# Another order for the chunk loop of a state-space and SwiGLU kernel, with a second adding transfer and phases read in order

## The chip, the cores and the metric

The kernel runs on one core of a Trainium2 chip. Time is device time in microseconds (us) for one launch; the median of several runs is compared, and a lower one is better. One further execution of each kernel was profiled, and all rows of traces come from it.

The engines work at their own pace and meet through semaphores: PE (TensorE, matrix products; PEld is its weight load), DVE (VectorE, elementwise), ACT (ScalarE, functions such as exp and sin), POOL (GpSimd; here mostly the issuer of DMA transfers) and SP (SyncE, the issuer of most transfers). Each executes its own instructions strictly in the order in which the program gives them.

## The reference

Two layers, each a diagonal state-space convolution and a SwiGLU block, with residuals:

```python
def _A_ref(u, A_re, A_im, B_re, B_im, C_re, C_im, log_dt, Dskip):
    dt = jnp.exp(log_dt)[:, None]
    A, Bc, Cc = A_re + 1j * A_im, B_re + 1j * B_im, C_re + 1j * C_im
    logdA, dB = dt * A, dt * Bc
    P = jnp.exp(logdA[:, :, None] * l[None, None, :])       # l = 0 .. L-1
    K = jnp.einsum("dn,dnl,dn->dl", Cc, P, dB).real
    ...                                                     # y = causal convolution of u with K
    return y + u * Dskip
for _ in range(2):
    x = x + _A_ref(_layernorm(x), ...)
    n = _layernorm(x)
    x = x + (silu(n @ w_gate) * (n @ w_up)) @ w_down
```

L = 2048 positions, D = 512 channels, N = 128 states, F = 1376. The kernel K (2048 lags for 512 channels) is the same in both layers.

## The kernel before

**Stages.** The head (0 to about 76 us) loads the inputs, makes the turns (phases as integers, a full turn being 2^32), normalizes the first block and transforms it, and prepares chunks 0 and 1. A loop over eight chunks of 64 channels (to about 300 us) makes K. What follows, some 900 us, splits the weights into halves of 16 bits, convolves in the frequency domain and runs the SwiGLU blocks; the change does not touch it.

**A chunk.** The powers for a lag are written as a product of a *large factor* (`re`, `im`: 65 columns for each channel, made by `gen_exp`, `gen_turns`, `gen_trig`, `gen_e`) and a *factor* `g` with 32 rows for each channel (`gen_g`). `lags` multiplies them on PE into `pk`; ACT copies `pk` out (`spread_in`, L499), transfers spread it over the partitions (`spread`), and `spectra` transforms it on PE, with copies on ACT (L550, L551), a sum on DVE (L553) and stores.

- `gen_turns` (DVE, L380 to L386): `xz` by a shift, then `tu`, 16 x 64 integers, by shifts and doubling sums. `gen_upper` (L407) adds the sixteenth row to all of `tu` in place, for the upper half.
- `gen_trig` (ACT): `xz` first, then the lower half (columns 33 to 48 of `re` and `im`: L399 the absolute value, L400 the sine, L401 the cosine), then, behind L407, the upper half (49 to 64) with the same three lines. L407 overwrites what the lower L399 and L400 read.
- `gen_exp` (ACT, L415 to L431): the moduli `mz` and the first 33 columns of `re`. `upper` (ACT, L425) squares them into `mu`.
- `gen_e` (DVE), seven steps: L440 twice, L443 twice, L445, L448 twice. The lags wait for the last.
- `gen_g` (DVE): L455 scales `xz`; L459 to L463 make row 0; then five doublings, each a product into the new rows (L469), a product into `tmp` (L480), and a sum (L483). The last doubling, 16 to 32, leaves its sum to a transfer in chunks 1 to 6: a product into `acc` (L472), then `G.dma_start(..., accum_op=OP.add)` (L473), issued by POOL, adds 1 MB to `g`. `acc` lies in the buffer of the other `g` (tags `ga` and `gb`), which the next chunk's `g` takes.

`take(it, n)` runs n steps of such a generator. In the head the order is written out. In the loop, each chunk c has a start on a list of moments (`starts`), and `prepare(c + 2)`, `factors(c + 1)`, `use(c)`, `second_block` (the first layer's second block, L289 on PE, L292 on ACT) and `weights` (sizes of the weights: loads by POOL at L317, squares on ACT at L323, column sums on PE, maxima on DVE at L329) put their steps on it with `at`. The list is sorted by moment and the instructions are given in that order; the moments only order them. PE, DVE, ACT and, in the loop, SP take this order as it is.

In the old order of one repetition, with `t` the chunk's start, DVE has: L455 to L460 (t + 0.2), L440 (0.3), L553 of the last chunk (2.1), the doublings with the second L440 in between (2.2 to 11.2, ending with L472), L380 to L386 for chunk c + 2 (14.4), L553 (17.3), L407 (21.5), then both L443, L445 and both L448 (22.0). ACT has: L425 (0.2), L499 (7.1), squares (8.0), `gen_exp` (12.6), L550 and L551 (14.0), squares (14.5), `xz` (17.4), L292 (17.6), the lower half (19.6), the upper (21.8), L593 (25.0), L550 and L551 (25.2).

Of the kernel before, what the change touches and what calls it, by code (L numbers as in the profile page):

```python
# [14 lines left out]
I32 = mybir.dt.int32  # L15
AF = mybir.ActivationFunctionType
OP = mybir.AluOpType
# [4 lines left out]
L, D, F = 2048, 512, 1376  # L22
P = 128
# [11 lines left out]
DC = 64  # L35
NCH = D // DC
# [37 lines left out]
def kernel(ctx, tc, x, a_re, a_im, b_re, b_im, c_re, c_im, log_dt, d_skip,  # L74
                           w_gate, w_up, w_down, c_ef, c_ei, c_ek, c_am, c_eh, c_eih, out):
    nc = tc.nc
    V, A, G, PE = nc.vector, nc.scalar, nc.gpsimd, nc.tensor
# [9 lines left out]
    def tl(shape, name, tag, dt=F32):  # L87
        return sb.tile(shape, dt, name=name, tag=tag, bufs=BUFS[tag])
# [106 lines left out]
    def stats(src, rows, scale, tag="stats", between=None, then=None):  # L195

        st = tl([P, 4, 6], "st", tag)
        mv = tl([P, 4, 2], "mv", tag)
        rs = tl([P, 8], "rs", tag)
        nb = rs[:, 4:]  # L200
        for r in range(rows):
            if between and r == 2:
                between()
            V.bn_stats(st[:, r], src[:, r])
            V.bn_aggr(mv[:, r], st[:, r])
        V.tensor_scalar(rs[:, :rows], mv[:, :rows, 1], EPS, 1.0 / scale ** 2, OP.add, OP.mult)
        G.tensor_tensor(rs[:, :rows], rs[:, :rows], mhalf[:, :rows], OP.pow)
        if then:
            then()
        V.scalar_tensor_tensor(nb[:, :rows], mv[:, :rows, 0], -1.0, rs[:, :rows], OP.mult, OP.mult)  # L210
        return rs, nb
# [147 lines left out]
        return re, im, mu, xz, mz, tu  # L359


    def turn_units(c0, c1):


        n = c1 - c0
        cs = slice(c0, c1)
        ft = tl([P, 2, 2, n], "ft", "sg")
        fr, fk = ft[:, 0], ft[:, 1].bitcast(I32)
        for i, scale in enumerate((1.0, 32.0)):
            V.scalar_tensor_tensor(fr[:, i], th[:, cs], scale / (2.0 * math.pi), dt[:, cs], OP.mult, OP.mult)  # L370
        A.activation(fk, fr, AF.Copy)
        V.tensor_tensor(fr, fr, fk, OP.subtract)
        for i, o in enumerate((th, th32)):
            V.tensor_scalar(o[:, cs].bitcast(I32), fr[:, i], TURN, TURN / 2 - 128.0, OP.mult, OP.min)

    def gen_turns(ch, ts):

        re, im, mu, xz, mz, tu = ts
        cs = slice(ch * DC, (ch + 1) * DC)
        V.tensor_tensor(xz[:, 1].bitcast(I32), th[:, cs].bitcast(I32).unsqueeze(1).to_broadcast([P, 5, DC]),  # L380
                        am.unsqueeze(2).to_broadcast([P, 5, DC]), OP.logical_shift_left)
        V.tensor_tensor(tu[:, 0:2], th32[:, cs].bitcast(I32).unsqueeze(1).to_broadcast([P, 2, DC]),
                        am[:, 0:2].unsqueeze(2).to_broadcast([P, 2, DC]), OP.logical_shift_left)
        yield
        for n in (2, 4, 8):
            V.tensor_tensor(tu[:, n:2 * n], tu[:, 0:n], tu[:, n - 1:n].to_broadcast([P, n, DC]), OP.add)  # L386
            yield
        G.memset(im[:, :, 32], 0.0)
        yield

    def gen_trig(ts):


        re, im, mu, xz, mz, tu = ts
        A.activation(xz[:, 2], xz[:, 1].bitcast(I32), AF.Sin, scale=-TWO_PI / TURN)
        tv = tu.rearrange("p m d -> p d m")
        for c, s, turns in ((xz[:, 0], xz[:, 1], xz[:, 1].bitcast(I32)), (re[:, :, 33:49], im[:, :, 33:49], tv),
                            (re[:, :, 49:65], im[:, :, 49:65], tv)):
            A.activation(c, turns, AF.Abs)  # L399
            A.activation(s, turns, AF.Sin, scale=TWO_PI / TURN)  # L400
            A.activation(c, c, AF.Sin, scale=-TWO_PI / TURN, bias=hpi)  # L401
            yield

    def gen_upper(ts):

        tu = ts[5]
        V.tensor_tensor(tu, tu, tu[:, 15:16].to_broadcast([P, 16, DC]), OP.add)  # L407
# [43 lines left out]
    def gen_g(ch, ts, g):  # L451

        re, im, mu, xz, mz, tu = ts
        w_ = w0[:, :, ch * DC:(ch + 1) * DC]
        V.tensor_tensor(xz, xz, mz.unsqueeze(1).to_broadcast([P, 3, 5, DC]), OP.mult)  # L455
        yield
        tmp8 = spare[0][:, :16 * DC].rearrange("p (i b d) -> p i b d", i=2, d=DC)
        tmp = tmp8
        V.tensor_tensor(g[:, :, 0], w_, re[:, :, 64].unsqueeze(1).to_broadcast([P, 2, DC]), OP.mult)  # L459
        V.tensor_tensor(tmp[:, :, 0], w_[:, ::-1], im[:, :, 64].unsqueeze(1).to_broadcast([P, 2, DC]), OP.mult)  # L460
        yield
        V.tensor_tensor(g[:, 0, 0], g[:, 0, 0], tmp[:, 0, 0], OP.subtract)
        V.tensor_tensor(g[:, 1, 0], g[:, 1, 0], tmp[:, 1, 0], OP.add)  # L463
        for n in (1, 2, 4, 8, 16):
            yield
            lv = n.bit_length() - 1
            zr = xz[:, 0:1, lv:lv + 1]
            zi = xz[:, 1:3, lv:lv + 1]
            V.tensor_tensor(g[:, :, n:2 * n], g[:, :, 0:n], zr.to_broadcast([P, 2, n, DC]), OP.mult)  # L469
            if n == 16 and 0 < ch < NCH - 1:  # L470
                tmp = tl([P, 2, 16, DC], "acc", ("gb", "ga")[ch % 2])
                V.tensor_tensor(tmp, g[:, ::-1, 0:16], xz[:, 2:0:-1, lv:lv + 1].to_broadcast([P, 2, 16, DC]), OP.mult)  # L472
                G.dma_start(g[:, :, 16:32].rearrange("p i b d -> p i (b d)"), tmp.rearrange("p i b d -> p i (b d)"),  # L473
                            accum_op=OP.add)
                continue
            step = min(n, 8)
            for b0 in range(0, n, step):
                tmp = tmp8[:, :, :step]
                o = slice(n + b0, n + b0 + step)
                V.tensor_tensor(tmp, g[:, :, b0:b0 + step], zi.to_broadcast([P, 2, step, DC]), OP.mult)  # L480
                if b0 + step == n:
                    yield
                V.tensor_tensor(g[:, :, o], g[:, :, o], tmp[:, ::-1], OP.add)  # L483
        yield
# [130 lines left out]
    def take(it, n):  # L615
        for _ in range(n):
            next(it, None)
# [302 lines left out]
    ts = [None] * (NCH + 2)  # L920
# [15 lines left out]
    with tc.manual_schedule(engines={mybir.EngineType.Activation, mybir.EngineType.DVE, mybir.EngineType.PE}):  # L936
# [2 lines left out]

        def turns():  # L940
            V.tensor_tensor(rho, rho, dt, OP.mult)
            turn_units(0, P)
            take(ex, 14)
            take(gen_turns(0, ts[0]), 5)
        stats_x = stats(xe, 4, 1.0, between=turns)
        tr = gen_trig(ts[0])
        take(tr, 2)
        gen_upper(ts[0])
        take(tr, 1)
        take(ex, 11)  # L950
        turn_units(P, D // 2)
        turn_units(D // 2, D)
        gen_w()
        norm_early(xe, ne, stats_x)
        fw = [direct(0, h, q, [ne[:, c, h * HD:(h + 1) * HD] for c in range(4)]) for h in range(2) for q in QORD]
        for f in fw:
# [7 lines left out]
        upper(ts[0])  # L964
        take(fw[0], 1)
        take(fw[1], 1)
        stats_x = stats(x1, 4, 1.0)
        take(fw[2], 1)
        for g in (gg, ge, gg, ge, gg, ge, gg, ge, gg, tn, gg, tn, gg, tn, gg, tn, gg, tn):
            take(g, 1)  # L970
        tr = gen_trig(ts[1])
        take(tr, 2)
        gen_upper(ts[1])
        for c in range(4):
            A.activation(x1[:, c], x1[:, c], AF.Identity, scale=stats_x[0][:, c:c + 1], bias=stats_x[1][:, c:c + 1])
        take(fw[3], 1)
# [17 lines left out]
        def at(t, f, n=1):  # L994
            plan.append((t, len(plan), (lambda: take(f, n)) if hasattr(f, "__next__") else f))

        def later(make):

            yield from make()

        def prepare(c, t):

            def tiles():
                ts[c] = gen_tiles(c)
            at(t + 0.4, tiles)
            steps = {k: later(lambda g=g: g(c, ts[c])) for k, g in
                     (("turns", gen_turns), ("exp", gen_exp))}
            tr = later(lambda: gen_trig(ts[c]))
            for k in range(5):
                at(t + 14.4 + 0.4 * k, steps["turns"])  # L1010
            for k in range(3):
                at(t + 17.4 + 2.2 * k, tr)
            at(t + 21.5, lambda: gen_upper(ts[c]))
            at(t + 12.6, steps["exp"], 100)

        def factors(c, t):

            at(t + 0.2, lambda: upper(ts[c]))

            def tiles():  # L1020
                gs[c] = tl([P, 2, 32, DC], "g", ("ga", "gb")[c % 2])
            at(t + 0.1, tiles)
            gg, ge = later(lambda: gen_g(c, ts[c], gs[c])), later(lambda: gen_e(ts[c]))
            for k in range(4):
                at(t + 0.2 + 2 * k, gg, 2)
                if k < 2:
                    at(t + 0.3 + 2 * k, ge, 1)
            for k in range(5):
                at(t + 8.2 + k, gg)
            at(t + 22.0, ge, 100)  # L1030

        def use(c, t):
# [215 lines left out]
```

## Time and profile before

| | |
|---|---|
| median of 3 runs | 1213.85 us (1213.76 to 1214.39) |
| profiled execution, its own time | 1216.14 us |
| its span, first to last instruction | 1214.3 us |
| PE busy | 1097.5 us, 90% of the span |
| DVE busy | 1007.3 us, 83% |
| ACT busy | 623.5 us, 51% |
| POOL busy | 92.8 us, 8% |
| chain that ended last | PE 35%, DVE 27%, issue 4%, DMA 4%, ACT 2% |

In the rows below, `L472 DVE TENSOR_TENSOR acc<-g,xz 128x2048` is the instruction of line 472, on DVE, from the tiles `g` and `xz` into `acc`, with the shape of what it writes. A row of a timeline has start, duration, engine, line, operation and count, and in brackets how long the engine had stood idle and what it had waited for. A row of the waits has the total, the number of times and the longest. A row of the groups has the busy time and the mean in ns of one instruction. A stretch has its length, the busy time of PE, weight loads, DVE, ACT and POOL with counts, the granted PE clock, the share of the DMA engines' time and GB/s. Consecutive instructions of an engine overlap by about 0.1 us in the records, so that the distance of two starts (a slot) is what one adds to a queue.

### The profile page before, as it was taken

To read this page: it belongs to the slowest core of one execution; us is meant where nothing else is said; L and a number is where in the kernel's file an instruction comes from. 1 tells how busy PE (TensorE), PEld (TensorE's weight loads), DVE (VectorE), ACT (ScalarE), POOL (GpSimd) and SP (SyncE) were. 2 spreads that over 40 slices of the span, in tenths; PEclk is the share of its full clock that TensorE was granted. 3 is DMA by queue.
4 is the path that set the end of the run, shared out by engine and by line. 5 is a ranking of instruction groups with operands and counts; after the bars stand their busy time and mean duration, and the time that the engine had idled before them with its cause. 6 is when DMAs were issued, how large, how long until landed. Compare 5 with 4: busy or idle time off the path is not lost.

```text
span 1214.3 us, 24571 instructions
## 1 busy us (share of the span) xinstructions
PE 1097.5 (90%) x10008; PEld 866.0 (71%) x10008; DVE 1007.3 (83%) x1612; ACT 623.5 (51%) x1205; POOL 92.8 (8%) x151
## 2 busy tenths in 40 slices
PE   0677888889989997999999999989999999999998
PEld 0555676767778684868687777858686776867875
DVE  3878888889879989899899999998997699984221
ACT  6398888993455255355745353564531553325111
POOL 1001111111000001001100000020100010000000
PEclk9988889889989999999999999999999999999999
DMA  5145665665748334732334444433435154312000
GB/s 207 44 149 129 144 142 151 152 174 165 256 140 260 118 117 144 183 116 92 86 113 141 124 157 129 133 102 116 124 120 152 60 133 132 117 57 45 14 23 18
DMA packets 136531, 151.17 MB, mean 124 GB/s; under 512 B 75473, under 2 KB 83665, under 8 KB 136418
## 3 DMA queue, kind: packets, MB, share of 16 engines
q1 hardware_dynamic: 129314, 126.47, 34.8%
q0 software_dynamic: 7104, 23.14, 7.3%
q8 instruction: 78, 1.28, 0.4%
q14 instruction: 35, 0.29, 0.1%
HBM read 101.85 MB, written 31.46 MB: 110 GB/s over the span
## 4 chain that ended last, share of the span: by engine, by line
PE 35%; DVE 27%; issue 4%; DMA 4%; ACT 2%; SPq 1%; POOL 0%; DVEq 0%; ACTq 0%; POOLq 0%
PE pgu L894 6%; PE pgu L895 6%; PE pgu L897 6%; DVE t L762 5%; DVE yk L765 4%; PE py L909 4%; PE py L910 4%; PE py L911 3%; PE pi L781 3%; PE pf L273 3%; DVE yk L762 2%; DMA mix<-nn 2%; DVE z L229 2%; DVE sg L901 2%; DVE bb L229 1%
## 5 line engine op out<-in xcount | busy, mean ns | idle before, releaser
L894 PE MATMUL pgu<-mix,wsl 128*128 128x256 f16 x1280 | 299.7, 273 | 5.3 <-DVE sg L901 2.7
L895 PE MATMUL pgu<-mix,wsl 128*128 128x256 f16 x1280 | 299.7, 273 | 0.0
L897 PE MATMUL pgu<-mix,wsl 128*128 128x256 f16 x1280 | 195.7, 273 | 0.0
L909 PE MATMUL py<-wsl,hh 128*128 128x512 f16 (+1 forms) x352 | 134.3, 381 | 8.8 <-DVE xg L914 7.1
L895 PEld LDWEIGHTS <-wsl 128*128 128x128 f16 x1280 | 125.5, 98 | 22.7 <-issue 6.5
L894 PEld LDWEIGHTS <-wsl 128*128 128x128 f16 x1280 | 125.3, 98 | 16.2
L897 PEld LDWEIGHTS <-wsl 128*128 128x128 f16 x1280 | 125.3, 98 | 15.0
L911 PE MATMUL py<-wsl,hl 128*128 128x512 f16 (+1 forms) x352 | 134.3, 382 | 0.3 <-DVE hl L903 0.3
L910 PE MATMUL py<-wsl,hh 128*128 128x512 f16 x320 | 122.0, 381 | 0.0
L762 DVE TENSOR_TENSOR t<-uu,w 128x1024 f32<-128x1024 f32 x96 | 117.7, 1226 | 2.7 <-DMA w<-wdr 2.5
L765 DVE TENSOR_TENSOR yk<-yk,t 128x1024 f32<-128x1024 f32 x96 | 117.7, 1226 | 0.3
L900 ACT ACTIVATE sg<-pgu,sc 128x512 f32<-128x512 f32 x80 | 54.6, 683 | 119.7 <-PE pgu L897 115.1
L901 DVE SCALAR_TENSOR_TENSOR sg<-pgu,sc,sg 128x512 f32<-128x512 f32 x80 | 60.3, 753 | 55.5 <-ACT sg L900 55.3
L523 PE MATMUL pw<-kt,ek 128*128 128x256 f32 (+1 forms) x384 | 93.6, 381 | 0.0
L902 ACT ACTIVATE hh<-sg 128x512 f16<-128x512 f32 x80 | 50.1, 626 | 77.2 <-DVE sg L901 77.1
L781 PE MATMUL pi<-yl,mix 128*128 128x256 f16 x576 | 78.9, 273 | 5.0 <-DVE yl L229 2.7
L493 PE MATMUL pk<-re,g 128*32 128x64 f32 x1024 | 46.2, 275 | 38.0 <-DVE re L448 33.1
L523 PEld LDWEIGHTS pw<-kt,ek 128*128 128x128 f32 x384 | 70.8, 194 | 8.3
L273 PE MATMUL pf<-z,eh 128*128 128x256 f16 x576 | 74.9, 273 | 0.0
L762 DVE TENSOR_TENSOR yk<-u,w0r 128x1024 f32<-128x1024 f32 x56 | 68.7, 1226 | 1.5 <-ACT u L275 1.5
L493 PEld LDWEIGHTS pk<-re,g 128*32 128x32 f32 x1024 | 41.0, 149 | 39.4 <-issue 39.4
L903 DVE TENSOR_TENSOR hl<-sg,hh 128x512 f16<-128x512 f32 x80 | 55.6, 696 | 15.4 <-ACT hh L902 15.3
(240 smaller groups left out, 2169.2 us busy)
## 6 DMA issues: line engine op xcount, KB each, us to landing
w<-wdr SPq DMA_DIRECT2D x96, 256.0 KB, 2.7
uu<-udr SPq DMA_DIRECT2D x96, 256.0 KB, 3.0
udr<-u POOLq DMA_DIRECT2D x32, 256.0 KB, 2.5
g<-acc POOLq DMA_DIRECT2D x6, 1024.0 KB, 9.0
udr<-u SPq DMA_DIRECT2D x16, 256.0 KB, 2.9
n<-ndr SPq DMA_DIRECT2D x16, 256.0 KB, 4.3
n<-xdr SPq DMA_DIRECT2D x4, 1024.0 KB, 5.7
kdr<-ks SPq DMA_DIRECT2D x6, 512.0 KB, 2.7
```

Of the source, the lines that this page charges most:

```text
L273: PE.matmul(pf[:, o], lhsT=e, rhs=m, start=k == 0, stop=k == len(terms) - 1)
L493: PE.matmul(o, lhsT=g[:, 0, :, d], rhs=re[:, d, 0:64], start=True, stop=False, tile_position=(0, 32 * grp))
L523: PE.matmul(pw[:, i], lhsT=e, rhs=kt[:, :, c + 4 * k0:4 * k1:4, :].rearrange("p g k d -> p k g d"), start=c == 0, stop=c == 3)
L762: V.tensor_tensor(t, uu.unsqueeze(1).to_broadcast([P, 2, 2, HD]), w.unsqueeze(2).to_broadcast([P, 2, 2, HD]), OP.mult)
L765: V.tensor_tensor(yk, yk, t, OP.add)
L781: PE.matmul(pi[:, o], lhsT=e, rhs=m, start=k == 0, stop=k == len(terms) - 1)
L894: PE.matmul(o, lhsT=wgu(wi, k, 0)[:, fs], rhs=nh[:, k], start=k == 0, stop=False)
L895: PE.matmul(o, lhsT=wgu(wi, k, 1)[:, fs], rhs=nh[:, k], start=False, stop=False)
L897: PE.matmul(o, lhsT=wgu(wi, k, 0)[:, fs], rhs=nlo[:, k], start=False, stop=k == 3)
L909: PE.matmul(py[:, r], lhsT=hh[:n, f, rc], rhs=wd(f, 0)[:n], start=f == 0, stop=False)
L910: PE.matmul(py[:, r], lhsT=hh[:n, f, rc], rhs=wd(f, 1)[:n], start=False, stop=False)
L911: PE.matmul(py[:, r], lhsT=hl[:n, f, rc], rhs=wd(f, 0)[:n], start=False, stop=f == FT - 1)
```

## The change

- `gen_trig` reads `tu` in the order in which it lies and writes `re` and `im` with a stride of one channel (65 elements), for L399 and L400. L401 keeps its order.
- `gen_g` hands the sum of the doubling 8 to 16 to an adding transfer as well, in chunks 1 to 6 (512 KB, from `tmp8`, issued by POOL).
- In these chunks both L440 and both L443 come behind that transfer's issue, then L407, and then the last doubling, which reads the rows that the transfer adds to. L445 and L448 stay at the end.
- In the loop the turns for chunk c + 2 go to the chunk's beginning, between steps of `gen_g`; ACT does `xz` and the lower half ahead of `gen_exp`, the upper half behind it.
- In the head the turns are cut at column 64 instead of 128 and 256, the second part begins before ACT's first exponentials; `gen_w` (the products of B, C and dt) comes before `gen_upper`; the turns of chunk 1 come in one piece before the statistics of the second block, and some steps of `gen_g` behind `gen_upper`.

```diff
-    def turn_units(c0, c1):
+    def turn_units(ft, c0, c1):
...
         A.activation(fk, fr, AF.Copy)
+        yield
         V.tensor_tensor(fr, fr, fk, OP.subtract)
...
-        tv = tu.rearrange("p m d -> p d m")
-        for c, s, turns in ((xz[:, 0], xz[:, 1], xz[:, 1].bitcast(I32)), (re[:, :, 33:49], im[:, :, 33:49], tv),
-                            (re[:, :, 49:65], im[:, :, 49:65], tv)):
+        rows = [[t[:, :, 33 + m:49 + m].rearrange("p d m -> p m d") for t in (re, im)] for m in (0, 16)]
+        for c, s, turns in ((xz[:, 0], xz[:, 1], xz[:, 1].bitcast(I32)), (*rows[0], tu), (*rows[1], tu)):
             A.activation(c, turns, AF.Abs)
             A.activation(s, turns, AF.Sin, scale=TWO_PI / TURN)
+            c = c.rearrange("p m d -> p d m") if turns is tu else c
             A.activation(c, c, AF.Sin, scale=-TWO_PI / TURN, bias=hpi)
...
-            if n == 16 and 0 < ch < NCH - 1:
-                tmp = tl([P, 2, 16, DC], "acc", ("gb", "ga")[ch % 2])
-                V.tensor_tensor(tmp, g[:, ::-1, 0:16], xz[:, 2:0:-1, lv:lv + 1].to_broadcast([P, 2, 16, DC]), OP.mult)
-                G.dma_start(g[:, :, 16:32].rearrange("p i b d -> p i (b d)"), tmp.rearrange("p i b d -> p i (b d)"),
+            if n >= 8 and 0 < ch < NCH - 1:
+                tmp = tmp8 if n == 8 else tl([P, 2, 16, DC], "acc", ("gb", "ga")[ch % 2])
+                V.tensor_tensor(tmp, g[:, ::-1, 0:n], xz[:, 2:0:-1, lv:lv + 1].to_broadcast([P, 2, n, DC]), OP.mult)
+                G.dma_start(g[:, :, n:2 * n].rearrange("p i b d -> p i (b d)"), tmp.rearrange("p i b d -> p i (b d)"),
                             accum_op=OP.add)
...
-            turn_units(0, P)
+            take(first, 1)
             take(ex, 14)
+            take(others, 1)
+            take(first, 1)
             take(gen_turns(0, ts[0]), 5)
+        ft = tl([P, 2, 2, D], "ft", "ga")
+        first, others = turn_units(ft, 0, DC), turn_units(ft, DC, D)
...
         take(tr, 2)
+        take(others, 1)
+        gen_w()
         gen_upper(ts[0])
         take(tr, 1)
         take(ex, 11)
-        turn_units(P, D // 2)
-        turn_units(D // 2, D)
-        gen_w()
         norm_early(xe, ne, stats_x)
...
+        take(tn, 5)
         stats_x = stats(x1, 4, 1.0)
         take(fw[2], 1)
-        for g in (gg, ge, gg, ge, gg, ge, gg, ge, gg, tn, gg, tn, gg, tn, gg, tn, gg, tn):
-            take(g, 1)
         tr = gen_trig(ts[1])
         take(tr, 2)
+        for g in (gg, ge, gg, ge, gg, ge, gg, ge, gg, gg):
+            take(g, 1)
         gen_upper(ts[1])
+        take(gg, 3)
...
-            for k in range(5):
-                at(t + 14.4 + 0.4 * k, steps["turns"])
-            for k in range(3):
-                at(t + 17.4 + 2.2 * k, tr)
-            at(t + 21.5, lambda: gen_upper(ts[c]))
+            for t0 in (0.3, 2.3, 2.5, 4.3, 6.3):
+                at(t + t0, steps["turns"])
+            at(t + 8.2, tr, 2)
+            at(t + 13.0, lambda: gen_upper(ts[c]))
+            at(t + 17.0, tr)
...
+            late = 0 < c < NCH - 1
             for k in range(4):
                 at(t + 0.2 + 2 * k, gg, 2)
-                if k < 2:
+                if k < 2 and not late:
                     at(t + 0.3 + 2 * k, ge, 1)
             for k in range(5):
-                at(t + 8.2 + k, gg)
+                at(t + (8.2 + k if k < 2 or not late else 15.0 + 0.5 * k), gg)
+            at(t + (9.6 if late else 22.0), ge, 4)
             at(t + 22.0, ge, 100)
```

More of the change, by code (lines that the diff above doesn't have):

```diff
@@ L359, in gen_tiles @@
         return re, im, mu, xz, mz, tu
-    def turn_units(c0, c1):
-        n = c1 - c0
+    def turn_units(ft, c0, c1):
         cs = slice(c0, c1)
-        ft = tl([P, 2, 2, n], "ft", "sg")
-        fr, fk = ft[:, 0], ft[:, 1].bitcast(I32)
+        fr, fk = ft[:, 0, :, cs], ft[:, 1, :, cs].bitcast(I32)
         for i, scale in enumerate((1.0, 32.0)):
@@ L374, in turn_units @@
             V.tensor_scalar(o[:, cs].bitcast(I32), fr[:, i], TURN, TURN / 2 - 128.0, OP.mult, OP.min)
+        yield
     def gen_turns(ch, ts):
@@ L1004, in tiles @@
                 ts[c] = gen_tiles(c)
-            at(t + 0.4, tiles)
+            at(t + 0.25, tiles)
             steps = {k: later(lambda g=g: g(c, ts[c])) for k, g in
```

## The prediction

> **What bounds the kernel now.** I read, in this order: the busy time by stretch, the waits of the first 400 us, and the timelines of VectorE (DVE), ScalarE (ACT) and TensorE (PE) side by side in one repetition of the chunk loop. Of each the lines that carry it: two of the page, two stretches, three waits (total, times, longest).
>
> ```profile
> span 1214.3 us, 24571 instructions
> PE   0677888889989997999999999989999999999998
> ...
> 13.00:28.00 15.00, 0.00 (x0) 0.00 (x0) 6.31 (x17) 14.75 (x26) 1.03 (x1) 1.00 0.47 179
> 137.00:168.00 31.00, 25.97 (x346) 22.27 (x347) 26.59 (x34) 27.27 (x56) 4.86 (x9) 0.89 0.62 152
> ...
> DVE tu L407 <- ACT im L400: 27.2, 8, 4.3
> DVE ft L372 <- ACT ft L371: 9.0, 3, 7.8
> PE pk L493 <- DVE re L448: 33.1, 6, 8.1
> ```
>
> The 40 slices of the PE row are 30 us each. The change touches what runs in the first ten; from there on PE is at nine tenths or more in nearly every slice, on results of the loop, so a shift of the loop's end should be a shift of the end. The stretches give the busy us of PE, weight loads, DVE, ACT and POOL in turn. Between 13 and 28 us PE does nothing, DVE 6.3 of 15 us, ACT 14.75: the head waits on ACT. From 137 to 168, about one repetition of the loop, PE, DVE and ACT have 26 to 27 us of work each in 31: no engine is full. The waits say why: a ring. DVE's L407 waits for ACT's L400 (eight times, 3.4 us each), PE's L493 for DVE's L448 (six times, 5.5 us each), and ACT's L499 for PE, as its rows further down show.
>
> ```profile
> 142.79 1.16 DVE L455 TENSOR_TENSOR xz<-xz,mz 128x960 f32<-128x960 f32 x1
> 143.86 0.40 DVE L459 TENSOR_TENSOR g<-w,re 128x128 f32<-128x128 f32 x1
> ...
> 154.45 1.23 DVE L483 TENSOR_TENSOR g<-g,spare 128x1024 f32<-128x1024 f32 x1
> ...
> 157.92 2.29 DVE L472 TENSOR_TENSOR acc<-g,xz 128x2048 f32<-128x2048 f32 x1
> 160.12 0.48 DVE L380 TENSOR_TENSOR xz<-th,am 128x320 int32<-128x320 int32 x1
> ...
> 162.23 0.95 DVE L553 TENSOR_TENSOR spare<-pw,spare 128x768 f32<-128x768 f32 x1
> 167.21 1.23 DVE L407 CUSTOM_DVE_ANT_0 tu<-tu 128x2048 uint16<-128x2048 uint16 x1 [4.03 <-ACT im L400]
> 168.35 2.36 DVE L443 TENSOR_TENSOR re<-re 128x1024 f32<-128x1024 f32 x2
> 170.62 2.22 DVE L445 SCALAR_TENSOR_TENSOR im<-im,mu 128x1984 f32<-128x1984 f32 x1
> 172.76 2.29 DVE L448 TENSOR_TENSOR re<-re,mu 128x992 f32<-128x992 f32 x2
> 174.96 1.16 DVE L455 TENSOR_TENSOR xz<-xz,mz 128x960 f32<-128x960 f32 x1
> ```
>
> One repetition is 32.2 us (142.79 to 174.96) with one idle time in it, the 4.0 us ahead of L407. Differences of starts below are "slots".
>
> **The head, part by part.** The turns are now cut after 64 columns, their two big leftovers started before ACT's exponentials instead of behind them, and the weights (L177 to L181) put ahead of L407.
>
> ```profile
> 19.13 0.16 DVE L210 SCALAR_TENSOR_TENSOR rs<-mv,rs 128x4 f32<-128x4 f32 x1 [1.23 <-POOL rs L207]
> 31.36 0.42 DVE L372 TENSOR_TENSOR ft<-ft 128x256 f32<-128x256 f32 x1 [7.80 <-ACT ft L371]
> 34.88 1.22 DVE L177 TENSOR_TENSOR bw<-bw,dt 128x1024 f32<-128x1024 f32 x1
> 39.73 1.91 DVE L281 TENSOR_SCALAR xne<-xne,rs 128x512 f32<-128x512 f32 x4
> 42.62 0.39 DVE L459 TENSOR_TENSOR g<-w,re 128x128 f32<-128x128 f32 x1
> 64.19 1.23 DVE L407 CUSTOM_DVE_ANT_0 tu<-tu 128x2048 uint16<-128x2048 uint16 x1 [2.77 <-ACT im L400]
> 75.79 0.36 PE L493 MATMUL pk<-re,g 128*32 128x64 f32 x7 [3.46 <-DVE g L483]
> 111.97 0.40 DVE L459 TENSOR_TENSOR g<-w,re 128x128 f32<-128x128 f32 x1
> 271.66 0.39 DVE L459 TENSOR_TENSOR g<-w,re 128x128 f32<-128x128 f32 x1
> ```
>
> The 448-column products ahead of L210 take DVE some 0.5 us more, so L210 is at 19.7. Then come the rest of the turns, 1.8 us (an estimate from L372's 0.42 for 256 elements), the weights 4.85 (34.88 to 39.73), L407 1.2: the norm (L281) starts at 27.5, not 39.73, and PE behind it 12.2 us earlier. ACT pays: its second half of the sines now starts behind the later L407, at 27.7, and lasts 4.8 (1.96 + 1.96 + 1.19 by the rows of L399 and L401 below, less overlap), so L459, which reads the last cosine, starts at 32.5, not 42.62. From L459 to the lags, 33.2 us to 75.79, the old order holds 3.9 us of waiting: 1.2 for POOL, as at L210, and 2.8 at L407. The new order keeps the first and, by ACT's list, about 0.9 of the second: 31.4. Lags at 63.9, the next L455 1.1 later (half of L448's pair) at 65.0.
>
> In the first repetition the new list gives the following L459 at 94.8 + s (65.0 + 1.1 for L455 + 19.3 + 9.4, as below, without one L553), s being DVE's wait for the new transfer: **17.2 − s us** ahead of 111.97.
>
> **The loop, part by part.** *Removed:* L483 for 8 to 16, 1.23, and the wait ahead of L407. *Moved:* L380 to L386 (2.11, 160.12 to 162.23) to the front, four large products (L440 twice, inside 143.86 to 160.12 already, and L443 twice, 2.27) and L407 (1.14) ahead of the last factor. From L459 to the end of L472's slot DVE then has 16.26 (143.86 to 160.12) − 1.23 + 2.11 + 2.27 + 1.14 = 20.5; interleaving takes out some 0.3 us of gaps between dependent instructions: 20.2. Behind L472 stay only L553, L445 and L448, 0.87 + 2.14 + 2.20 = 5.2, then L455.
>
> ```profile
> 160.50 1.23 POOL L473 DMA_DIRECT2D g<-acc  x1 [8.44 <-DVE acc L472]
> ...
> g<-acc POOLq DMA_DIRECT2D x6, 1024.0 KB, 9.0
> udr<-u POOLq DMA_DIRECT2D x32, 256.0 KB, 2.5
> ...
> DMA to landing us min/median/max: 2.6/5.0/10.3
> 120.00:125.00 5.00, 5.00 (x25) 3.84 (x24) 4.90 (x5) 4.97 (x27) 0.00 (x0) 1.00 1.01 223
> ```
>
> (POOL's timeline, two lines of the page's DMA issues with KB and us to landing, the landings of the weight loads of L317, one stretch with DMA share and GB/s at its end.) Here is **the wait that takes the old one's place**. The 1 MB adding transfer is issued 0.4 us behind L472's slot and lands 9.0 later: 9.4. Until now 14.8 us of DVE lay behind it (160.12 to 174.96), now 5.2. Its landing holds PE's lags, and L459 of the next chunk too, since acc lies in the buffer that next g takes. DVE reaches L459 at 6.3 and stands 3.1 us, with its whole queue. DVE and transfer alone give a repetition of 20.2 + 9.4 = **29.6 + s**.
>
> The new 512 KB transfer has L440 (as long as L443), L443 and L407, 5.7 us, to hide in. Its landing: 4.7 us on the line through 256 KB (2.5) and 1 MB (9.0); at least half of 9.0; at most 10.3, the longest of the weight loads on the same queue (the line of three numbers). Its bytes would move where now, as at 120 to 125, every DMA engine is busy (share 1.01) with the spread of the lags, stores and loads. I take 6.6, nearer the line than the ceiling: s = 0.4 + 6.6 − 5.7 = **1.3**, bounds 0 and 5.0. POOL's own queue: the transfer stands behind weight loads that wait for ACT's squares; by ACT's list these are issued some two us ahead of it, so I price that wait at nothing, and inside the upper bound if not.
>
> ```profile
> 110.17 0.47 PE L493 MATMUL pk<-re,g 128*32 128x64 f32 x8 [8.08 <-DVE re L448]
> 115.95 1.02 ACT L499 ACTIVATE ks<-pk 128x1024 f32<-128x1024 f32 x1 [2.68 <-PE pk L494]
> ...
> 148.77 1.02 ACT L499 ACTIVATE ks<-pk 128x1024 f32<-128x1024 f32 x1 [3.61 <-PE pk L494]
> 175.14 0.37 ACT L551 ACTIVATE w0r<-pw 128x256 f32<-128x256 f32 x1
> L399 ACT ACTIVATE re<-tu 128x1024 f32<-128x1024 int32 x16 | 31.4, 1964 | 4.6 <-DVE tu L386 3.2 <-DVE tu L407 1.4
> L401 ACT ACTIVATE re<-re,hpi 128x1024 f32<-128x1024 f32 x16 | 19.0, 1187 | 0.0
> L415 ACT ACTIVATE mz<-rho 128x64 f32<-128x64 f32 x40 | 6.7, 243 | 0.1
> L419 ACT ACTIVATE re<-rho 128x64 f32<-128x64 f32 x160 | 25.0, 305 | 0.0
> ```
>
> *ACT.* Read in order, written with a stride of 65 elements: L399 and L400 cost 1.96 us against 1.19 of L401, which strides neither way. But L419 only writes with that stride, and is 62 ns longer than L415 for 64 elements: 0.97 ns each, 1.0 us for 1024, as much as the strided read costs now. So I price the reordering at nothing: 0, bounds −0.8 and +0.2 us for each of four instructions. [...]
>
> ACT's list then stays: lags to L499 5.8 (110.17 to 115.95), L499 to the end of L551 26.6 (148.77 to 175.51, less 0.2 idle). Still two table loads, the first sine following a sine. L551 releases the L553 that now comes 1.2 us behind L459: 5.8 + 26.6 + (20.2 − 1.2) + 9.4 + s = 60.8 + s for two repetitions, or **30.4 + s/2**. With s = 1.3 the two are 30.9 and 31.05; I take 31.05. Five repetitions (111.97 to 271.66) took 159.7, 31.94 each: **−4.5 us**. PE's 26 us fit.
>
> **The last chunk** keeps its old order, but the lags ahead of it start with L459 (the transfer's landing) instead of with L455, 1.1 us sooner. Nothing lost if DVE sets the pace there, 1.1 if PE does; I take **+1.1**. Sum: −17.2 + 1.3 − 4.5 + 1.1 = **−19.3**. The profiled span goes from 1214.3 to 1195.0; that run took 1216.1 us, 2.3 above the median of the others, 1213.85, and against the median the forecast is 1194.6.
>
> **The rivals.** *The add lands late* (slower). For s above 1.6 the sum is −27.8 + 6s (head, five repetitions of 29.6 + s, tail): nothing is left from s = 4.6, a landing of 9.9 us. For it: a smaller transfer took 10.3, and DMA is full just there. Against: that load stood behind the 1 MB one, here at most loads of 172 to 256 KB do. At a landing of 11 us: s = 5.7, 1213.85 + 6.4 = 1220. *Strided writes are cheap*: ACT gets 0.8 us off four instructions, the head 1.6 us, the repetition 29.6 + s: −29.4 + 6s, −21.6 at s = 1.3: 1192; 1184.5 at s = 0. L419 is against it, though 62 ns may be latency. *The gain is given back behind the loop*: weights, loads and convolution from 300 us on could hold to something that does not move up; then 1206 to 1214. Against: all of it is issued behind the loop's own instructions.
>
> **How the numbers follow.** What I forecast 0.60; cheap writes 0.16; late add 0.14; given back 0.10. A change under 0.2%, 2.4 us, cannot be told from none. Late add is slower (0.13, 0.01 same), given back faster 0.06, same 0.03, slower 0.01: faster 0.82, same 0.04, slower 0.14. Range 1184.5 (cheap writes, s = 0) to 1208 (s = 3.7, a landing of 9.0 like that of 1 MB); the late add beyond it and part of the last case are left out.
>
> **What would show it.** Right: PE's first L289 at 28 us, L493 near 64; L407 without a wait in the loop, a wait of some 3 us at L459 ended by the transfer of acc, one of 1 to 2 us at the L469 of 2048 elements; L399 still near 1.95 us; starts of L380 about 31 us apart. Wrong: L399 near 1.1; no wait at L459; L469 waiting over 4 us; or the first L894 not some 19 us earlier.

## The result, and the profile after

The changed kernel takes 1222.71 us (median of 4 runs, 1221.21 to 1224.51) against 1214.12 of the kernel before on the same chip: ratio 1.0069, 95% interval 1.0049 to 1.0089. It is 8.6 us **slower**; forecast were 1194.6 and a range of 1184.5 to 1208. Its profiled execution took 1224.04 us, with a span of 1222.3. In this profile L398 and L399 are what L399 and L400 are in the profile before (absolute value and sine); L401, the cosine, and all other lines named below keep their numbers. One execution among all runs, the profiled one of sums_behind below, took 2292.63 us, and the ratio of that run leaves it out.

The page, first its span and busy times, then the 40 slices:

```profile
span 1222.3 us, 24568 instructions
...
PE 1109.3 (91%) x10008; PEld 866.8 (71%) x10008; DVE 999.3 (82%) x1601; ACT 627.1 (51%) x1206; POOL 99.6 (8%) x157
...
PE   1948988789888998999999999989999999999998
```

PE is busy 12 us longer than before (1097.5) with the same 10008 instructions: they have become slower, not more. The first slices are fuller (1948 for 0677), so the head did move.

DVE's timeline (start, us, engine, line, operation, tiles; in brackets the idle time ahead and what ended it):

```profile
26.98 1.91 DVE L281 TENSOR_SCALAR xne<-xne,rs 128x512 f32<-128x512 f32 x4
...
32.04 0.39 DVE L459 TENSOR_TENSOR g<-w,re 128x128 f32<-128x128 f32 x1 [2.09 <-ACT re L401]
...
65.39 1.15 DVE L455 TENSOR_TENSOR xz<-xz,mz 128x960 f32<-128x960 f32 x1
...
95.81 0.39 DVE L459 TENSOR_TENSOR g<-w,re 128x128 f32<-128x128 f32 x1 [3.89 <-DMA g<-acc]
...
273.21 0.39 DVE L459 TENSOR_TENSOR g<-w,re 128x128 f32<-128x128 f32 x1 [4.09 <-DMA g<-acc]
```

This divides the 8.0 us between the two spans. Up to the L459 of chunk 2 the new kernel **gains 16.2** (95.81 for 111.97). The next five repetitions take 177.4 us (95.81 to 273.21), 35.5 each, instead of 159.7: it **loses 17.7**. From the last L459 to the end it loses 6.5 more (949.1 for 942.6). The head did what was forecast of it; the loop did the opposite.

Where a repetition's time goes is in the waits between 95 and 275 us (total, times, longest):

```profile
POOL st L317 <- ACT sq L323: 64.7, 10, 12.1
...
PE nrm L326 <- ACT sq L323: 24.8, 5, 5.3
DVE g L459 <- DMA g<-acc: 22.7, 6, 4.7
ACT wo L550 <- PE pw L523: 18.6, 5, 4.4
...
DVE wo L553 <- ACT w0r L551: 12.6, 5, 4.3
DVE g L469 <- DMA g<-spare: 9.6, 5, 3.0
```

L407 is no longer among them, and the wait at L459 (3.8 us each) is about the one that the forecast put in its place. New and not forecast are four: PE's L326, a column sum for the weights' sizes, waits 5.0 us for ACT's squares (L323) in every repetition; POOL's weight loads (L317) wait 64.7 us for the same squares, 14.6 in this stretch before; ACT's L550 waits for PE's products; and DVE's L553 waits for ACT's L551, which stands behind that L550. The next two fences are ACT and PE in one repetition.

```profile
142.05 1.02 ACT L499 ACTIVATE ks<-pk 128x1024 f32<-128x1024 f32 x1 [2.60 <-PE pk L494]
...
145.79 2.08 ACT L398 ACTIVATE re<-tu 128x1024 f32<-128x1024 int32 x1
...
152.76 3.08 ACT L419 ACTIVATE re<-rho 128x64 f32<-128x64 f32 x20
...
158.40 1.26 ACT L323 ACTIVATE sq<-st 128x344 bf16<-128x344 f32 x3
```

```profile
158.96 1.20 PE L326 MATMUL nrm<-sq,onesb 128*128 128x344 bf16 x3 [4.90 <-ACT sq L323]
159.96 1.16 PE L523 MATMUL pw<-kt,ef 128*128 128x256 f32 x2
...
161.67 2.93 PE L523 MATMUL pw<-kt,ek 128*128 128x256 f32 x6
...
169.75 1.46 PE L523 MATMUL pw<-kt,ek 128*128 128x256 f32 x6
```

ACT now does the lower sines (L398 on) between L499 and the exponentials (L419), and the second group of squares stands behind all of it: they end 17.6 us after L499 starts (142.05 to 159.66). L326 needs them, and in PE's queue the products of L523 stand behind L326, and the next lags behind these. In the same repetition of the kernel before, the sums did not wait:

```profile
160.58 0.60 PE L326 MATMUL nrm<-sq,onesb 128*128 128x344 bf16 x3
...
161.90 1.56 PE L523 MATMUL pw<-kt,ek 128*128 128x256 f32 x6
```

The six records of one product set take 1.56 us there and 2.93 behind the wait. The stretches show why (busy us of PE, weight load, DVE, ACT, POOL; then the granted clock, DMA share and GB/s); first after, then before:

```profile
123.30:128.00 4.70, 4.66 (x11) 2.71 (x11) 4.55 (x5) 4.67 (x5) 2.97 (x4) 0.50 0.57 132
128.00:132.20 4.20, 4.20 (x11) 3.35 (x10) 2.56 (x3) 3.98 (x5) 0.00 (x0) 0.51 1.05 172
132.20:136.40 4.20, 4.20 (x23) 3.14 (x25) 1.30 (x4) 0.00 (x0) 0.00 (x0) 1.00 1.01 290
136.40:142.05 5.65, 4.62 (x257) 4.42 (x258) 4.28 (x13) 3.03 (x5) 0.03 (x1) 1.00 0.12 44
```

```profile
128.50:136.70 8.20, 8.20 (x38) 6.41 (x36) 4.95 (x9) 7.95 (x10) 2.95 (x4) 1.00 0.83 129
...
142.10:148.80 6.70, 6.70 (x257) 6.63 (x258) 6.63 (x13) 3.09 (x7) 0.06 (x1) 0.58 0.02 6
```

Five idle microseconds of PE are followed by seven to nine at **half clock** (0.50 and 0.51 from 123.3 to 132.2, 0.53 from 159 to 166 in the next repetition). Before, that stretch fell on the lags, which take 6.7 us at a clock of 0.58 and 5.7 at full clock (136.32 to 142.05 after the change): 1 us. The difference is small because at full clock PE is busy for only 4.6 of these us and stands for 1.0 in the middle, waiting for nothing that the profile shows. Now the slow stretch falls on the products, which take 11.8 us (124.5 to 136.3) instead of 8.2. So the ring in the repetition shown is: L499 to the end of the squares 17.6, L326 0.3, products 11.1 (159.96 to about 171.0), lags to L499 5.6, in all 34.6 us (142.05 to 176.64).

The squares hold POOL too. POOL's timeline after, and one line of the one before:

```profile
159.21 1.66 POOL L317 DMA_DIRECT2D st<-in_B_w_gate_dram  x3 [11.24 <-ACT sq L323]
160.83 1.30 POOL L473 DMA_DIRECT2D g<-acc  x1
```

```profile
161.23 2.19 POOL L317 DMA_DIRECT2D st<-in_B_w_gate_dram  x3
```

Before, the 1 MB transfer (the L473 at 160.50 shown with the prediction) was issued ahead of the weight loads; now it stands behind three that wait for squares, and goes out 2.8 us after DVE's L472 (155.85 plus a slot of 2.20, so 158.05); over the five repetitions it is 1.6 to 3.0.

### The profile page after: what moved, and what is told of

Same layout as the page of the kernel before. It is cut to its first block, busy times and chain, and to the rows that moved or that the text cites. A ratio compares the mean times of both kernels' runs of the same rounds, so it can differ in the third digit from the quotient of the medians.

```text
span 1222.3 us, 24568 instructions
## 1 busy us (share of the span) xinstructions
PE 1109.3 (91%) x10008; PEld 866.8 (71%) x10008; DVE 999.3 (82%) x1601; ACT 627.1 (51%) x1206; POOL 99.6 (8%) x157
## 4 chain that ended last, share of the span: by engine, by line
PE 37%; DVE 25%; DMA 4%; issue 4%; ACT 1%; SPq 1%; POOL 0%; DVEq 0%; ACTq 0%
PE pgu L894 6%; PE pgu L895 6%; PE pgu L897 6%; DVE t L762 5%; DVE yk L765 4%; PE py L909 4%; PE py L910 4%; PE py L911 3%; PE pi L781 3%; PE pf L273 3%; DVE yk L762 2%; DVE z L229 2%; DVE sg L901 2%; DMA mix<-nn 1%; DVE bb L229 1%
## 5 line engine op out<-in xcount | busy, mean ns | idle before, releaser
L897 PEld LDWEIGHTS <-wsl 128*128 128x128 f16 x1280 | 125.2, 98 | 14.6
L523 PE MATMUL pw<-kt,ek 128*128 128x256 f32 (+1 forms) x384 | 105.3, 416 | 0.0
L523 PEld LDWEIGHTS pw<-kt,ek 128*128 128x128 f32 x384 | 78.4, 214 | 11.9
L903 DVE TENSOR_TENSOR hl<-sg,hh 128x512 f16<-128x512 f32 x80 | 54.8, 686 | 16.0 <-ACT hh L902 15.9
L910 PEld LDWEIGHTS <-hh 128*128 128x128 f16 (+1 forms) x352 | 34.8, 99 | 45.8 <-issue 10.8
L781 PEld LDWEIGHTS <-mix 128*128 128x128 f16 x576 | 56.0, 98 | 12.8 <-issue 3.2
```

The lines of the kernel that those rows point to most:

```text
L523: PE.matmul(pw[:, i], lhsT=e, rhs=kt[:, :, c + 4 * k0:4 * k1:4, :].rearrange("p g k d -> p k g d"), start=c == 0, stop=c == 3)
L781: PE.matmul(pi[:, o], lhsT=e, rhs=m, start=k == 0, stop=k == len(terms) - 1)
L897: PE.matmul(o, lhsT=wgu(wi, k, 0)[:, fs], rhs=nlo[:, k], start=False, stop=k == 3)
L910: PE.matmul(py[:, r], lhsT=hh[:n, f, rc], rhs=wd(f, 1)[:n], start=False, stop=False)
```

## The experiments

"Repetition" is the mean of the five from the L459 of chunk 2 to that of chunk 7; the ratio is to the kernel before, run on the same chip beside each kernel (medians 1214.12, 1216.29, 1216.27 and 1215.0).

| kernel | median, us | ratio [95%] | repetition, us |
|---|---|---|---|
| before | 1214.12 | 1 | 31.94 |
| the change | 1222.71 | 1.0069 [1.0049, 1.0089] | 35.5 |
| head_only | 1202.51 | 0.9888 [0.9864, 0.9912] | 31.72 |
| squares_early | 1202.86 | 0.9887 [0.9865, 0.9910] | 31.87 |
| sums_behind | 1211.69 | 0.9960 [0.9946, 0.9975] | not read |
| sums_behind_2 | 1211.61 | 0.9968 [0.9952, 0.9985] | 32.85 |
| no_second_add | 1224.75 | 1.0061 [1.0039, 1.0082] | 35.26 |
| old_read | 1225.15 | 1.0086 [1.0059, 1.0113] | 36.16 |
| mixed_late_squares | 1221.63 | 1.0070 [1.0040, 1.0099] | 35.19 |
| warm | 1216.59 | 1.0008 [0.9996, 1.0020] | 34.93 |
| mixed | 1200.10 | 0.9878 [0.9853, 0.9902] | 31.33 |
| mixed_steps | 1191.58 | 0.9802 [0.9775, 0.9829] | 29.31 |

**squares_early** moves the squares of the second group ahead of the exponentials in ACT's list:

```diff
-            for k, t0, t1, t2, t3 in ((0, -1.4, 8.0, 13.9, 17.0), (1, 8.1, 14.5, 17.45, 19.5),
+            for k, t0, t1, t2, t3 in ((0, -1.4, 8.0, 13.9, 17.0), (1, 8.1, 10.0, 17.45, 19.5),
```

> The changed kernel with the other end of the same wait moved: ACT squares the second group of weights (L323) ahead of the exponentials instead of behind them; PE's list is as in the change. Theory (PE's queue): L323 ends some 7 us sooner, L326 does not wait, and the time is that of the run with the sums moved, 1200 to 1203, give or take 2. Rival (adding transfers): within 5 us of 1222. A third view, that the half clock of PE alone lengthens the products, would leave a repetition at 33 to 34 us and the time near 1213.

1202.86: one number in the program takes 22 us back (1.0069 less 0.9887, of 1214). PE's and POOL's timelines:

```profile
176.84 0.46 PE L326 MATMUL nrm<-sq,onesb 128*128 128x344 bf16 x2
...
178.02 1.56 PE L523 MATMUL pw<-kt,ek 128*128 128x256 f32 x6
```

```profile
145.58 1.66 POOL L317 DMA_DIRECT2D st<-in_B_w_gate_dram  x3 [4.71 <-ACT sq L323]
151.35 1.23 POOL L473 DMA_DIRECT2D g<-acc  x1 [4.11 <-DVE acc L472]
```

The sums of the second group (176.84) have no wait, the six records take 1.56 us, and the transfer waits for DVE's L472 alone. The granted clock of its profiled execution is 0.978 in the mean, against 0.967 of the change.

**sums_behind** leaves the squares late and puts L326 behind the products instead, so that PE no longer waits but POOL still does:

```diff
-            for k, t0, t1, t2, t3 in ((0, -1.4, 8.0, 13.9, 17.0), (1, 8.1, 14.5, 17.45, 19.5),
+            for k, t0, t1, t2, t3 in ((0, -1.4, 8.0, 13.9, 17.0), (1, 8.1, 14.5, 24.0, 27.0 if i == NCH - 2 else 36.0),
```

> The changed kernel, with one thing moved: PE's column sums of the second group of weights (L326, second of a chunk) stand behind the products of spectra instead of ahead of them, and their maximum with DVE later. Theory (PE's queue: those sums wait for ACT's squares, which the change put behind the sines and exponentials; the products and the next lags stand behind them): the wait of 5 us at L326 goes, the half clock of PE falls into the lags again, L550 and L553 hardly wait, and a repetition falls from 35.5 us to about 31, the forecast's ring of DVE and the 1 MB transfer. Five repetitions and a part: 20 to 23 us less than the changed kernel, 1200 to 1203, faster than before by 11 to 14. Rival (the two adding transfers set the repetition, by the waits at L459 and L469): a repetition stays within 1 us of 35.5, and the time within 5 us of 1222.

1211.69: 13 us of the 22 (1.0069 less 0.9960), a miss by 9. Its profile is that of the execution of 2292.63 us, so the same kernel ran again:

> The same kernel as sums_behind, for its profile. Theory (PE's queue): L326 of the second group no longer waits for L323, the products of L523 take 8 us at full clock instead of 12, and the 9 us by which this kernel missed 1202 stand in one later place, the loads of the next weights, which are issued behind the sums (POOL's L317 or PE's next use of them): repetitions near 33.7 us, 1209 to 1212. Rival (the half clock falls on the products whatever stands ahead of them): products still 11 to 12 us long, with no wait at L326.

1211.61, with repetitions of 32.85 us instead of the expected 33.7, and the profile shows what is left. POOL's and PE's timelines:

```profile
183.10 1.12 POOL L317 DMA_DIRECT2D st<-in_B_w_gate_dram  x2 [11.11 <-ACT sq L323]
184.19 1.29 POOL L473 DMA_DIRECT2D g<-acc  x1
```

```profile
177.77 0.59 PE L523 MATMUL pw<-kt,ef 128*128 128x256 f32 x2
...
185.79 0.46 PE L326 MATMUL nrm<-sq,onesb 128*128 128x344 bf16 x2
192.50 0.47 PE L493 MATMUL pk<-re,g 128*32 128x64 f32 x8 [6.26 <-DMA g<-acc]
```

The products take 8.0 us (177.77 to 185.79), as in the kernel before at a clock of 1.00 (8.2), so the rival falls. What holds the lags is the adding transfer: L472 starts at 179.69 and its slot ends at 181.9, the transfer is issued at 184.19, 2.3 us later, behind the loads. Of the two places that I had named, PE's use of the late weights is not it; POOL's loads are, through the transfer that stands behind them. The ring by POOL here is 18.3 us from L499 to the issue, 8.3 to the lags and 6.6 to the next L499, in all 33.2 (165.92, 184.19, 192.50, 199.14).

**warm** keeps the changed order and fills PE's idle time with useless work, the second block's products again:

```diff
-        for i in range(2):
+        for i in halves:
...
-        return direct(1, h, q, n, space)
+        return direct(1, h, q, n, space, (0, 1, 0, 1, 0))
```

> The changed kernel with useless work ahead of the wait: each second-block product of L289 (16 matmul records, 3.5 us) is computed two and a half times, so that PE is busy for 5.2 us of the 5 us that it stood in front of L326. Theory (the wait costs twice: it makes PE idle, and the products behind it run at half clock): L326 ends when it did, 18.2 us behind L499, its products take 8 us instead of 12, and repetitions go from 35.5 to between 32 and 33.5: 1206 to 1213, faster than the changed kernel though PE does more. Rival (the products are slow for another reason, their operands or the transfers, and PE's idle time has no part in it): 1220 to 1226.

1216.59, between the two and outside the expected 1206 to 1213: 0.9996 to 1.0020 of the kernel before, against 1.0049 to 1.0089 of the change. PE's timeline:

```profile
157.17 0.97 PE L326 MATMUL nrm<-sq,onesb 128*128 128x344 bf16 x3
...
159.01 1.56 PE L523 MATMUL pw<-kt,ek 128*128 128x256 f32 x6
...
167.26 0.34 PE L493 MATMUL pk<-re,g 128*32 128x64 f32 x6 [0.96 <-DMA g<-acc]
...
172.03 0.31 PE L493 MATMUL pk<-re,g 128*32 128x64 f32 x4 [2.24 <-issue]
```

The part on the clock came out: with PE kept busy L326 ends when it did, the product records are back at 1.56 us, and the products end 9.1 us behind its start (157.17 to 166.3) instead of 12. The gain of 2 to 3.5 us a repetition did not: the lags then wait for the adding transfer, which POOL issued at 158.95 and whose data DVE and PE had 8.2 us later, and they stop for 2.2 us in the middle, for nothing that the profile shows. Such a stop is in each of the change's five repetitions too, 1.1 us in the mean, and 2.1 here; its cause is open. The ring by POOL is 18.8 + 8.3 + 8.0 = 35.1 us in this repetition (L499 at 140.15, issue 158.95, lags 167.26, L499 at 175.26). So two rings through L323 lie close together, one by PE (34.6 in the change), one by POOL and the transfer; shortening one brings up the other. sums_behind and squares_early say the same from the other side.

**no_second_add** takes the new 512 KB transfer back (L480 and L483 for 8 to 16 return), all else as changed:

```diff
-            if n >= 8 and 0 < ch < NCH - 1:
+            if n == 16 and 0 < ch < NCH - 1:
```

> The changed kernel without the new 512 KB transfer: the sum of the doubling 8 to 16 is DVE's again (1.25 us a chunk, six chunks), in the changed order; L469 of the last doubling waits for nothing. Theory (PE's queue): PE sets the repetition, so DVE's 1.25 us more and its 1.6 us of waiting less show in the waits at L459 and L553 only; time within 3 us of 1222. Rival (adding transfers): the wait at L469, 10.3 us in all, and its share in the DMA engines go; 5 to 10 us less, 1212 to 1217.

**old_read** takes the reordered sines back:

```diff
...
-        rows = [[t[:, :, 33 + m:49 + m].rearrange("p d m -> p m d") for t in (re, im)] for m in (0, 16)]
+        tv = tu.rearrange("p m d -> p d m")
...
```

> The changed kernel with the sines read with the stride and written in order, as before. Theory (writing with the stride costs about what reading with it costs, and PE's queue sets the pace): L398 and L399 back to 1.96 us from 2.08, at most 0.3 us of a repetition, 1220 to 1224. Rival (the new order of the strided side is what slows the loop, through ACT's list): 1212 or less.

**mixed_late_squares** takes both back and the late last factor too:

```diff
...
-                at(t + (8.2 + k if k < 2 or not late else 15.0 + 0.5 * k), gg)
-            at(t + (9.6 if late else 22.0), ge, 4)
+                at(t + 8.2 + k, gg)
...
```

> The changed head and the changed places of turns, sines and L407 in the loop, but the strided read, the second adding transfer and the later last factor taken back. L323 of the second group still stands behind the exponentials in ACT's list. Theory (PE's queue at L326 alone makes the loop slow): L326 waits for L323 in most repetitions, repetitions of 35 to 36 us, 1217 to 1224. Rival (the late last factor with its transfer, ahead of L459, makes it slow): no more than 32 us, 1203 or less.

All three stay as slow as the change: 1224.75, 1225.15 (a little above the expected 1220 to 1224) and 1221.63, with repetitions of 35.2 to 36.2 us. The wait at L326 is in each, here no_second_add's and mixed_late_squares' rows of the waits between 95 and 280 us and 95 and 275:

```profile
PE nrm L326 <- ACT sq L323: 24.7, 5, 5.2
```

```profile
PE nrm L326 <- ACT sq L323: 25.4, 5, 5.3
```

So neither the second adding transfer nor the order in which the phases are read makes the loop slow. The early place of turns and sines does, by what it pushes back. mixed_late_squares says one thing more. In three of its five repetitions the 1 MB transfer is issued at once, ahead of the loads that wait, as in this row of POOL's timeline:

```profile
153.76 1.23 POOL L473 DMA_DIRECT2D g<-acc  x1 [8.32 <-DVE acc L472]
```

L472 starts at 151.18 there. The three repetitions still take 35.1 us in the mean (96.08 to 201.38), so the wait at PE is enough without POOL's queue.

**head_only** is the kernel before with the head's part of the change alone (turns cut after 64 columns, leftovers ahead of the exponentials, weights ahead of L407, the new list of steps); the loop is untouched:

```diff
-            turn_units(0, P)
+            take(first, 1)
             take(ex, 14)
+            take(others, 1)
+            take(first, 1)
...
```

> The kernel before with the head of the change alone (turns cut at column 64, the weights' products ahead of L407, chunk 1's turns in one piece); the loop, the phases' order and the single adding transfer as before. Both theories: the lags of chunk 0 start near 64.5 us instead of 75.8, the stall of 3.5 us at L440 in the first repetition goes, and the loop keeps its 31.9 us; 12 to 15 us less than before, 1199 to 1202. If the head's lead is given back in the loop, then 1208 or more.

1202.51, half a microsecond above the expected. Its L459 of chunk 2 starts at 96.28, 15.7 us ahead of before, and its repetitions stay at 31.7. The head is worth 13.6 us (1 less 0.9888, of 1214); the loop as changed costs 22 (1.0069 less 0.9888), and repaired by squares_early it is worth nothing.

**mixed** goes for the rest: mixed_late_squares with the squares early. The turns, L380 to L386 and L407, stay in front, the factor has its old order, and the 1 MB transfer has more DVE work behind it.

```diff
-            for k, t0, t1, t2, t3 in ((0, -1.4, 8.0, 13.9, 17.0), (1, 8.1, 14.5, 17.45, 19.5),
+            for k, t0, t1, t2, t3 in ((0, -1.4, 8.0, 13.9, 17.0), (1, 8.1, 10.0, 17.45, 19.5),
```

> As mixed_late_squares, with L323 of the second group moved ahead of the exponentials, as in squares_early. Theory: L326 does not wait. The 1 MB adding transfer (9 us) has L443, L407, L553, L445 and L448 behind it, 8.7 us of DVE, so L459 waits 1 us at most: DVE's ring is 29 us, ACT's about as long, and the kernel comes to 1188 to 1195. Rival (something else holds a repetition at 31.8, as squares_early and head_only have it, whatever the order in the loop): 1201 to 1204.

1200.1: neither. Between 95 and 275 us its waits name two things that hold DVE and PE:

```profile
DVE spare L553 <- ACT w0r L551: 16.2, 5, 4.1
PE pk L493 <- ACT u L292: 12.0, 3, 4.1
```

DVE's L553 stood ahead of both L443 and waited for ACT; the lags waited for L292, which stood behind ACT's upper sines. **mixed_steps** moves these two steps and nothing else:

```diff
-                                      (n + 6.9, n + 14.0, n + 17.3, n + 22.0))))[:2 if c < NCH - 2 else 1]:
+                                      (n + 6.9, n + 14.0, n + 22.1, n + 22.3))))[:2 if c < NCH - 2 else 1]:
...
-            at(t + 22.0, ge, 100)
+            at(t + 22.0, ge, 2)
+            at(t + 22.2, ge, 100)
...
-            at(t + 17.6, lambda: take(box[0], 1))
+            at(t + 16.9, lambda: take(box[0], 1))
```

> As mixed, and two waits of its profile moved: L553 of the third and fourth quarter behind L443 (it stood 2.5 to 3.6 us for ACT's L551 ahead of it) and L292 of the second block ahead of the upper sines (PE's lags stood 4 us for it). Theory (these two hold mixed at 31.3 us a repetition): repetitions of 28.5 to 29.5, 1186 to 1194. Rival (ACT's list is full and takes the gain back at another place): 1197 to 1202.

1191.58, and the wait for L292 is gone from the same stretch of the waits, that of L553 is small:

```profile
DVE spare L553 <- ACT w0r L551: 3.1, 3, 2.1
```

The repetition is 29.3 us, 0.9802 of the kernel before, with the old factor, no second transfer and the old strided read. It beats both kernels.

## Why the prediction was wrong

**The head was right.** L281 at 26.98 (27.5 forecast), L459 at 32.04 (32.5), L455 at 65.39 (65.0), the L459 of chunk 2 16.2 us sooner (17.2 − s, with s = 1.3: 15.9). Measured alone, 13.6 us of it reach the end.

**The transfers were right in kind and nearly in size.** DVE waits for the 512 KB transfer 1.9 us each time between 95 and 275 us (9.6 / 5; s = 1.3 forecast, bounds 0 and 5.0), and at L459 3.8 us for the 1 MB one (3.1 forecast). That the second comes out so near is in part luck: the transfer took 8.1 us to land and not 9.0, but was issued 1.6 to 3.0 us behind L472's slot and not 0.4. The DMA issues from 95 to 280 us, with KB and us to landing:

```profile
g<-acc POOLq DMA_DIRECT2D x5, 1024.0 KB, 8.1
g<-spare POOLq DMA_DIRECT2D x5, 512.0 KB, 6.9
```

6.6 had been taken for the smaller. "The add lands late" did not decide: without that transfer the kernel is as slow.

**Strided writes** cost here what strided reads cost, and a little more; groups by line, mean ns ahead of the second bar's idle time, after and then old_read:

```profile
L399 ACT ACTIVATE im<-tu 128x1024 f32<-128x1024 int32 x16 | 33.5, 2097 | 0.1
L398 ACT ACTIVATE re<-tu 128x1024 f32<-128x1024 int32 x16 | 33.1, 2072 | 3.6 <-DVE tu L407 3.6
```

```profile
L399 ACT ACTIVATE re<-tu 128x1024 f32<-128x1024 int32 x16 | 32.2, 2015 | 3.6 <-DVE tu L407 3.6
L400 ACT ACTIVATE im<-tu 128x1024 f32<-128x1024 int32 x16 | 32.0, 1999 | 0.1
```

2.07 and 2.10 us against 2.0 in old_read and 1.96 before, inside the bound of +0.2, so the reading of L419 held, and "strided writes are cheap" fell.

**The step that failed is "PE's 26 us fit".** It weighed PE's *work* against the repetition and priced PE at nothing. PE's *place* was what counted. By the new order of ACT's list the lower sines push the second group of squares back, and no step of the forecast asked what waits for these squares on PE: L326, with the products, the next lags and ACT's L550 behind it. On POOL, where L317 waits for them, it asked only about the smaller transfer. Even at full clock the ring by PE, 17.6 + 0.3 + 8.2 + 5.7 = 31.8 us, would have been longer than the 31.05 of the forecast; the half clock on the products adds about 3. In place of −4.5 for five repetitions came +17.7, and moving L323 alone takes 22 us back.

**POOL's queue** was priced for the 512 KB transfer only ("I price that wait at nothing"); it was the 1 MB one that came to stand behind the loads and went out 1.6 to 3.0 us behind L472's slot after the change, 0.4 to 3.5 in sums_behind_2. What this alone is worth is not shown: squares_early is 9 us faster than sums_behind, but the two differ in ACT's list as well as in POOL's queue, and only 4.9 of the 9 us lie in the five repetitions (32.85 against 31.87 each).

**The loop's −4.5 was not there even when repaired.** squares_early runs at 31.87 us a repetition, not 31.05: ACT's squares now stand ahead of L551, and one of DVE's two L553 waits for L551 three times in five, 9.3 us in all, the other four times, 3.8. Whether these waits alone make the 0.8 us was not tried.

**The tail** was forecast at +1.1 and came to +6.5. Of these, 4.1 lie between L459 and the last chunk's L499 (281.58 − 273.21 = 8.4 after, 275.91 − 271.66 = 4.3 before): the lags there stand behind the last slow products (a clock of 0.50 from 265 to 271, 0.73 from 271 to 273), not behind L459. The other 2.4 come behind L499, where before, the change, squares_early, warm and head_only took between 937.6 and 941.6 us to the end. The longest is head_only, which has the loop of before, so 2.4 us lie within what these profiles differ by anyway, and whether they belong to the change is open. So of "the gain is given back behind the loop" at most this much is true.

## What to carry to other kernels

When a step is moved ahead on one engine, list what it pushes back there, and for each of these who waits for it and what is queued behind the waiter, on every engine and on the queue that issues transfers: here a small square on ACT held PE's products and a 1 MB transfer at once. An engine with spare work in sum can still set the pace by one early instruction that waits. Where one wait is removed and the gain is missing, look for a second ring of nearly the same length; measure parts alone, since here the head's gain and the loop's loss together looked like a small loss.

## What was not expected of the hardware

PE's idle time cost twice here. After 5 us without work the granted clock is 0.50 to 0.51 from 123.3 to 132.2 and 0.53 from 159 to 166 in the next repetition, seven to nine us, and products take 2.93 us for six records instead of 1.56. The lags, 64 elements wide, lose only 1 us in 6.7 (a clock of 0.58 before, 1.00 after), since at 1.00 they have the stop of 1.0 us. In the kernel before, the lags behind waits of 4.8 to 8.1 us show a mean clock of 0.57 to 0.75 over 5.7 to 6.8 us, so 3.4 to 5.7 us at half clock by an estimate: the slow stretch in front of the lags was shorter. Useless products that kept PE busy put the clock of these stretches back to 1.00 (busy times, clock, DMA share and GB/s by stretch, in warm):

```profile
152.00:157.00 5.00, 5.00 (x25) 4.41 (x24) 4.61 (x3) 4.97 (x21) 0.00 (x0) 1.00 0.03 6
...
159.00:161.00 2.00, 2.00 (x10) 1.79 (x10) 2.00 (x3) 1.98 (x2) 1.25 (x1) 1.00 0.86 256
```

What sets the length of the slow stretches is not shown.
